# The end of a transformer layer on one core: residual by an identity matmul, copies on ScalarE, and the first FFN1 blocks in halves

## The chip, the cores and the metric

The kernel runs on one core of a Trainium2 chip. That core has five engines that run side by side and meet at semaphores: TensorE (PE in the profile, its weight loads are PEld), VectorE (DVE), ScalarE (ACT), GpSimd (POOL), and SyncE (SP), which issues the DMA transfers here. The metric is device time in microseconds (us), the median of several runs.

## The reference

One layer on x of 2048 tokens by 1024, in bf16: attention with 32 heads of 32, then a feed-forward block of width 3584, each behind a layer norm and each added to its input.

```python
x = A_x
h = x + _A_ref(_layernorm(x, axis=-1), A_wqkv, A_wo)      # attention, then @ wo
h2 = h + _B_ref(_layernorm(h, axis=-1), B_w1, B_b1, B_w2, B_b2)
# _B_ref: gelu(x @ w1 + b1) @ w2 + b2
```

What matters below is the second half for one chunk of tokens: `h = x + attention @ wo`, the layer norm of h, `h @ w1` with gelu (FFN1), and `@ w2` plus h (FFN2).

## The kernel before, in words

**Tiling.** The tokens are handled in four chunks (`qc`) of 512, each of four tiles (`t4`) of 128. Attention of chunk qc runs while the projection by wo, layer norm, FFN1 and FFN2 of chunk qc-1 run as background work of TensorE, in one bank of PSUM (bank 7) and with matmuls in four column strips (line 439). After the attention of the last chunk nothing is left to run beside it: the last chunk's wo, norm, FFN1 and FFN2 come alone, lines 896 to 905. This is the tail. It may use all eight PSUM banks (the list `al`), and its matmuls are whole ones, 128 rows by 128 columns of weights with 512 moving columns (line 443).

**The tail, stage by stage.**

- `finish` (lines 665 to 681): when the last pair of heads is done, VectorE copies the denominators (Dsb, line 666) and the sums (Osb, line 668) out of PSUM, takes reciprocals in four pieces of 128 tokens (line 673), and multiplies (line 677) to give OT, the attention output of head group 7, one piece for each tile of tokens.
- `wo` (lines 703 to 721): for each tile and each half j of the 1024 columns, eight matmuls (one for each head group g) into one bank, then one VectorE addition (line 719) that takes the bank and the tile of x from memory (`b_xr`) and writes `hch`, in bf16.
- `ln2` (lines 723 to 733): for each tile, two statistics instructions (line 487) and one that joins them (489) on VectorE; four small steps on GpSimd (492 to 498: copy, add epsilon, two powers), one small copy on VectorE (493), then the normalization on VectorE (502). Eight transposes on TensorE (508) go to one bank, and one ScalarE copy (512) writes the tile's part of `hnT`.
- `ffn1` (lines 735 to 761): 14 blocks of w1 with 256 columns each, in a ring of four buffers (`b_w1r`); each block gives two groups `fc` of eight matmuls over all 512 tokens. A group needs the `hnT` of all four tiles. Gelu by group: ScalarE adds the bias (751), VectorE squares and multiplies (754, 756), ScalarE takes tanh (758), VectorE makes gT (760). Their buffers are rings of four.
- `ffn2` (lines 763 to 785): for each j and t4, a bias matmul, then 28 matmuls over gT, then one VectorE instruction (782) and the store.

**What sets the order.** The code does not write engine queues by hand. Every instruction becomes a task with a cost and a priority; `Graph.schedule` (lines 98 to 178) plays the tasks through a model of the engines and so fixes the order of each engine's queue, and `assign` (181 to 250) gives each task the semaphore waits that it needs. On the chip each queue runs in that order: an instruction that waits holds up all that stand behind it on its engine. Dependencies are by buffer: `hch` is one buffer for each tile, so its second half is written after the first, and the statistics of a tile wait for both halves.

Of the kernel before, what the change touches and what calls it, by code (L numbers as in the profile page):

```python
# [7 lines left out]
ACT = mybir.ActivationFunctionType  # L8
ALU = mybir.AluOpType
# [3 lines left out]
P = 128  # L13
# [271 lines left out]
def build_kernel(nc, A_x, A_wqkv, A_wo, B_w1, B_b1, B_w2, B_b2, out):  # L285
# [5 lines left out]
    NCH = S // 512  # L291
    G = D // P
    DC = D // P
    FC = F // P
    SCALE = DH ** -0.5
    EPS_BF = 1.0013580322265625e-05
    C2 = 1.0 / 0.044715
    K2 = 2.0 * math.sqrt(2.0 / math.pi) * 0.044715

    x2 = A_x[0]  # L300
# [34 lines left out]
    ident, B_ident = sb(top, "ident", [P, P], BF)  # L335
# [84 lines left out]
    def c_dve_ps(n):  # L420
        return (120 + n) / 960.0 + 0.02

    def c_dve(n, x=1):
        return (62 + n / x) / 960.0 + 0.02
# [7 lines left out]
    def mm(bank, lhsT, rhs, start, stop, reads, narrow, cols=(0, 512)):  # L432

        c0, c1 = cols
        occ = MM * (c1 - c0) / 512.0 + 0.003
        if narrow:
            fns = []
            for j in range(4):
                fns.append(lambda p, j=j: p.matmul(psum[32 * j:32 * j + 32, bank, c0:c1], lhsT[:, 32 * j:32 * j + 32], rhs,  # L439
                                                   start=start, stop=stop, tile_position=(0, 32 * j), skip_group_check=True))  # L440
            pe(fns, occ, reads=reads, writes=[B_ps[bank]], mode="col")
        else:
            pe(lambda p: p.matmul(psum[:, bank, c0:c1], lhsT, rhs, start=start, stop=stop),  # L443
               occ, reads=reads, writes=[B_ps[bank]], mode="full")

    def act(fn, n, reads=(), writes=(), prio=0, ap_bias=False, kind=""):
        return gr.add(E.Activation, fn, c_act(n, ap_bias), 0.14, reads, writes, prio, kind)

    def dve(fn, occ, reads=(), writes=(), prio=0):
        return gr.add(E.DVE, fn, occ, 0.08, reads, writes, prio)  # L450
# [4 lines left out]
    def dma(out_ap, in_ap, nbytes, reads=(), writes=(), prio=0, noncontig=False, after=()):  # L455
        def fn(s):
            if noncontig:
                with nc.allow_non_contiguous_dma(reason="strided gather"):
                    return s.dma_start(out_ap, in_ap)
            return s.dma_start(out_ap, in_ap)  # L460
        return gr.add(E.SP, fn, 0.06, 0.0, reads, writes, prio, nbytes=nbytes, after=after)
# [147 lines left out]
    class Att:  # L609
# [55 lines left out]
        def finish(self, qc, g, pr, bank):  # L665
            dve(lambda v: v.tensor_copy(Dsb[64 * pr:64 * pr + 64, :], psum[64:128, bank, :]), c_dve_ps(512),  # L666
                reads=[B_ps[bank]], writes=B_Dsb[pr], prio=-1)
            dve(lambda v: v.tensor_copy(Osb[64 * pr:64 * pr + 64, :], psum[0:64, bank, :]), c_dve_ps(512),  # L668
                reads=[B_ps[bank]], writes=[B_Osb[pr]], prio=-1)
            self.fin.add((qc, g, pr))  # L670
            if (qc, g, 1 - pr) in self.fin:
                for k in range(4):
                    dve(lambda v, k=k: v.reciprocal(Dsb[:, 128 * k:128 * k + 128], Dsb[:, 128 * k:128 * k + 128]), 0.93,  # L673
                        reads=[B_Dsb[0][k], B_Dsb[1][k]], writes=[B_Dsb[0][k], B_Dsb[1][k]], prio=1)
                    if qc == NCH - 1 and g == G - 1:
                        c = slice(128 * k, 128 * k + 128)
                        dve(lambda v, c=c: v.tensor_tensor(OT[:, qc % 2, g, c], Osb[:, c], Dsb[:, c], ALU.mult), c_dve(128),
                            reads=[B_Dsb[0][k], B_Dsb[1][k]] + B_Osb, writes=[B_OT[qc % 2][g][k]], prio=1)
                if not (qc == NCH - 1 and g == G - 1):
                    dve(lambda v: v.tensor_tensor(OT[:, qc % 2, g, :], Osb[:, :], Dsb[:, :], ALU.mult), c_dve(512),  # L680
                        reads=B_Dsb[0] + B_Dsb[1] + B_Osb, writes=B_OT[qc % 2][g], prio=1)
# [16 lines left out]
    def wblock(R, src_ap, prio=1):  # L698
        s = R.next("w1", R.nw1)
        dma(R.w1[:, s, :, :], src_ap.rearrange("(dc p) c -> p dc c", p=P), P * DC * 512, writes=[R.B_w1[s]], prio=prio)  # L700
        return s

    def wo(R, qc, banks, RX):
        nb = 0
        R.cnt["w1"] += -R.cnt["w1"] % 4
        ws = [wblock(R, A_wo[:, 256 * k:256 * k + 256]) for k in range(4)]
        assert ws == [0, 1, 2, 3]
        for t4 in range(4):
            for j in range(2):
                s = ws[2 * j]  # L710
                bank = banks[nb % len(banks)]
                nb += 1
                tt = qc * 4 + t4
                for k, g in enumerate([7, 0, 1, 2, 3, 4, 5, 6] if len(banks) == 1 else range(G)):
                    mm(bank, OT[:, qc % 2, g, t4 * P:(t4 + 1) * P], R.w1[:, s:s + 2, g, :], k == 0, k == 7,
                       [B_OT[qc % 2][g][t4], R.B_w1[s], R.B_w1[s + 1]], len(banks) == 1)
                x3 = RX.next("x", RX.nx)
                dma(RX.x[:, x3, :], x2[tt * P:(tt + 1) * P, 512 * j:512 * j + 512], P * 1024, writes=[RX.B_x[x3]], prio=1)
                dve(lambda v, t4=t4, j=j, x3=x3, bank=bank: v.tensor_tensor(  # L719
                    hch[:, t4, 512 * j:512 * j + 512], psum[:, bank, :], RX.x[:, x3, :], ALU.add),  # L720
                    c_dve_ps(512), reads=[B_ps[bank], RX.B_x[x3]], writes=[B_hch[t4]])

    def ln2(R, qc, banks, between=None):
        nb = 0
        for t4 in range(4):
            if t4 == 2 and between is not None:
                between()
            s = R.next("xb", R.nxb)
            layer_norm([(hch[:, t4, :], B_hch[t4], R.xb[:, s, :], R.B_xb[s])], 1)
            bank = banks[nb % len(banks)]  # L730
            nb += 1
            transposes(R.xb[:, s, :], R.B_xb[s], bank, R.hnT[:, :, t4 * P:(t4 + 1) * P], R.B_hnT[t4],
                       "dve" if len(banks) == 1 else "act", 0)

    def ffn1(R, qc, banks):
        nb = 0
        for blk in range(FC // 2):
            s = wblock(R, B_w1[:, 256 * blk:256 * blk + 256])
            for f in range(2):
                fc = 2 * blk + f  # L740
                bank = banks[nb % len(banks)]
                nb += 1
                for dc in range(DC):
                    mm(bank, R.w1[:, s, dc, f * P:(f + 1) * P], R.hnT[:, dc, :], dc == 0, dc == DC - 1,
                       [R.B_w1[s]] + R.B_hnT, len(banks) == 1)
                i = R.next("gl", R.ngl)
                if len(banks) == 1:
                    dve(lambda v, i=i, fc=fc, bank=bank: v.tensor_scalar(R.xh[:, i, :], psum[:, bank, :], b1f[:, fc:fc + 1], None, ALU.add),  # L748
                        c_dve_ps(512), reads=[B_ps[bank], B_b1f], writes=[R.B_xh[i]])
                else:  # L750
                    act(lambda a, i=i, fc=fc, bank=bank: a.activation(R.xh[:, i, :], psum[:, bank, :], ACT.Identity,
                                                                      bias=b1f[:, fc:fc + 1], scale=1.0),
                        512, reads=[B_ps[bank], B_b1f], writes=[R.B_xh[i]], ap_bias=True)
                dve(lambda v, i=i: v.tensor_tensor(R.sq[:, i, :], R.xh[:, i, :], R.xh[:, i, :], ALU.mult), c_dve(512, 2),
                    reads=[R.B_xh[i]], writes=[R.B_sq[i]], prio=1)
                dve(lambda v, i=i: v.scalar_tensor_tensor(R.uu[:, i, :], R.sq[:, i, :], C2, R.xh[:, i, :], ALU.add, ALU.mult),
                    c_dve(512), reads=[R.B_sq[i], R.B_xh[i]], writes=[R.B_uu[i]], prio=1)
                act(lambda a, i=i: a.activation(R.th[:, i, :], R.uu[:, i, :], ACT.Tanh, bias=0.0, scale=K2 / 2), 512,
                    reads=[R.B_uu[i]], writes=[R.B_th[i]], prio=-1)
                dve(lambda v, i=i, fc=fc: v.scalar_tensor_tensor(gT[:, fc, :], R.th[:, i, :], 1.0, R.xh[:, i, :], ALU.add, ALU.mult),  # L760
                    c_dve(512), reads=[R.B_th[i], R.B_xh[i]], writes=[B_gT[fc]], prio=1)

    def ffn2(R, qc, banks):
        nb = 0
# [135 lines left out]
    R2.w2, R2.B_w2, R2.nw2, R2.cnt["w2"] = R1.w2, R1.B_w2, R1.nw2, R1.cnt["w2"]  # L900
    R2.hnT, R2.B_hnT = R1.hnT, R1.B_hnT
    wo(R1, NCH - 1, al, R2)
    ln2(R2, NCH - 1, al)
    ffn1(R2, NCH - 1, al)
    ffn2(R2, NCH - 1, al)


# [99 lines left out]
```

## Time and profile before

| what | before |
|---|---|
| median of 3 runs | 1203.71 us |
| lowest, highest | 1203.57, 1204.14 us |
| span of the profiled execution | 1417.9 us |
| mean granted TensorE clock in the profiled execution | 0.749 |
| TensorE, ScalarE, VectorE, GpSimd busy | 96%, 77%, 47%, 3% |
| from the last attention matmul to the end | 1256.8 to 1415.8 us |

The profiled execution has no other time than its span, and the span is 17.8% longer than the median of the runs. The trace says that TensorE was granted three quarters of its clock for nearly all of it. The trace is of that one execution; the runs have no trace.

How to read the views: a row of the chain of waits gives start, duration, engine, what is written and the line, and how many instructions were merged. A row of the timeline adds the shapes and, in square brackets, the engine's idle time before the row and what ended it. A row of the table by stretches gives, for each engine, its busy time and the number of instructions in that stretch, then the granted clock and the traffic of the DMA engines.

### The profile page before, as it was taken

The numbers are of one execution on the slowest core, as the hardware profiler recorded it, in microseconds if no ns is written. First come the engines' busy times: TensorE is split into PE (matmuls) and PEld (weight loads), VectorE is DVE, ScalarE is ACT, GpSimd is POOL, SyncE is SP. The second block draws the span as 40 slices with busy tenths as digits, with TensorE's granted clock in tenths as the row PEclk, the third lists the DMA queues.
The fourth block names the chain that finished last, engine by engine and source line by source line (L and its number), as shares of the span: only waits on it lengthen the run. The fifth ranks groups of instructions, "written<-read, shape, count | busy, mean of one in ns | idle before, by whom it ended". The sixth has DMA issues, their size and how long they took to land.

```text
span 1417.9 us, 37847 instructions
## 1 busy us (share of the span) xinstructions
PE 1366.2 (96%) x17326; PEld 510.9 (36%) x17336; DVE 673.2 (47%) x1165; ACT 1085.3 (77%) x1189; POOL 37.9 (3%) x96
## 2 busy tenths in 40 slices
PE   8999999999999999999999999999999999978999
PEld 5544443433333333332333333333333333324333
DVE  7354444443546774223547762225677612245710
ACT  4778787878888888888888888888988888844500
POOL 2000000000100000000100000000000000001000
PEclk7777777777777777777777777777777777766777
DMA  6800000025343222303342230422323322202222
GB/s 165 224 2 13 28 13 14 13 72 156 101 122 101 76 69 72 124 16 98 107 124 71 83 98 16 124 71 63 107 73 98 102 66 85 87 0 75 74 93 71
DMA packets 165793, 112.29 MB, mean 79 GB/s; under 512 B 25345, under 2 KB 162817, under 8 KB 164866
## 3 DMA queue, kind: packets, MB, share of 16 engines
q1 hardware_dynamic: 165634, 109.87, 26.2%
q8 instruction: 136, 2.23, 0.7%
q14 instruction: 23, 0.19, 0.1%
HBM read 98.58 MB, written 11.27 MB: 77 GB/s over the span
## 4 chain that ended last, share of the span: by engine, by line
PE 91%; ACT 4%; DVE 3%; issue 1%; POOL 1%; DMA 0%; POOLq 0%; DVEq 0%
PE ps L439 48%; PE ps L654 17%; PE ps L634 12%; PE ps L443 10%; ACT PT L643 3%; PE ps L658 2%; PE ps L798 1%; ACT xnT L512 1%; DVE a_xh L748 1%; PE ps L508 1%; DVE V L606 0%; DVE stg L547 0%; DVE Osb L668 0%; DVE Dsb L666 0%; DMA a_w1r<-in_A_wqkv_dram 0%
## 5 line engine op out<-in xcount | busy, mean ns | idle before, releaser
L643 ACT ACTIVATE PT<-ps 128x1024 bf16<-128x1024 f32 x1024 | 989.2, 1025 | 180.5 <-PE ps L634 166.1
L654 PE MATMUL ps<-PT,V 128*32 128x512 bf16 x2048 | 383.4, 457 | 13.7 <-DVE V L606 6.2
L658 PE MATMUL ps<-PT,ones 128*32 128x512 bf16 x2048 | 384.8, 458 | 0.0
L439 PE MATMUL ps<-a_w2r,gT 128*32 128x512 bf16 x2688 | 241.9, 452 | 0.0
L634 PE MATMUL ps<-QT,KT 32*128 32x512 bf16 x2048 | 216.7, 414 | 7.4 <-ACT PT L643 7.3
L439 PE MATMUL ps<-a_hnT,a_w1r 128*32 128x512 bf16 x2688 | 215.2, 454 | 4.0 <-DVE a_xh L748 3.2
L654 PEld LDWEIGHTS ps<-PT,V 128*32 128x32 bf16 x2048 | 103.3, 104 | 143.9 <-issue 89.3
L634 PEld LDWEIGHTS ps<-QT,KT 32*128 32x128 bf16 x2048 | 51.5, 91 | 272.3 <-ACT PT L643 164.5
L439 PE MATMUL ps<-xnT,Wall 128*32 128x512 bf16 x1344 | 111.6, 453 | 7.0 <-ACT xnT L512 4.8
L439 PEld LDWEIGHTS ps<-a_w2r,gT 128*32 128x32 bf16 x2688 | 77.3, 109 | 112.0 <-issue 103.3
L673 DVE RECIPROCAL Dsb<-Dsb 128x128 f32<-128x128 f32 x128 | 115.1, 928 | 1.0
L439 PEld LDWEIGHTS ps<-a_hnT,a_w1r 128*32 128x32 bf16 x2688 | 70.6, 107 | 108.0 <-issue 71.4
L782 DVE SCALAR_TENSOR_TENSOR a_ost<-ps,hch 128x512 bf16<-128x512 f32 x24 | 16.6, 692 | 189.8 <-PE ps L439 189.7
L658 PEld LDWEIGHTS ps<-PT,ones 128*32 128x32 bf16 x2048 | 103.5, 104 | 6.6 <-issue 6.6
L748 DVE TENSOR_SCALAR a_xh<-ps,b1f 128x512 bf16<-128x512 f32 x84 | 63.1, 751 | 81.3 <-PE ps L439 80.2
L666 DVE COPY Dsb<-ps 64x512 f32<-64x512 f32 x64 | 44.4, 694 | 101.5 <-PE ps L658 100.1
L439 PE MATMUL ps<-Wall,xnT 128*32 128x256 bf16 x2048 | 83.8, 314 | 0.0
L547 DVE CAST stg<-ps 128x512 bf16<-128x512 f32 x40 | 27.5, 689 | 89.2 <-PE ps L439 89.2
L443 PE MATMUL ps<-a_hnT,b_w1r 128*128 128x512 bf16 x219 | 64.5, 470 | 2.1 <-ACT a_hnT L512 1.5
L439 PEld LDWEIGHTS ps<-Wall,xnT 128*32 128x32 bf16 x2048 | 57.6, 107 | 22.7 <-issue 11.3
L443 PE MATMUL ps<-a_w2r,gT 128*128 128x512 bf16 x219 | 64.1, 461 | 0.5
L439 PE MATMUL ps<-a_w1r,OT 128*32 128x512 bf16 x768 | 63.1, 453 | 0.8 <-DVE hch L719 0.5
(69 smaller groups left out, 875.5 us busy)
## 6 DMA issues: line engine op xcount, KB each, us to landing
a_w2r<-in_B_w_dram SPq DMA_DIRECT2D x56, 512.0 KB, 4.6
a_w1r<-in_B_w_dram SPq DMA_DIRECT2D x42, 512.0 KB, 3.9
a_w1r<-in_A_wo_dram SPq DMA_DIRECT2D x16, 512.0 KB, 4.7
QT<-q_scratch SPq DMA_DIRECT2D x60, 128.0 KB, 2.8
b_w1r<-in_B_w_dram SPq DMA_DIRECT2D x14, 512.0 KB, 3.8
a_w1r<-in_A_wqkv_dram SPq DMA_DIRECT2D x11, 512.0 KB, 5.1
xrb<-in_A_x_dram SPq DMA_DIRECT2D x16, 256.0 KB, 3.9
Wall<-in_A_wqkv_dram SPq DMA_DIRECT2D x16, 256.0 KB, 5.4
```

The lines of the kernel that those rows point to most:

```text
L439: fns.append(lambda p, j=j: p.matmul(psum[32 * j:32 * j + 32, bank, c0:c1], lhsT[:, 32 * j:32 * j + 32], rhs, start=start, stop=stop, tile ...
L443: pe(lambda p: p.matmul(psum[:, bank, c0:c1], lhsT, rhs, start=start, stop=stop), occ, reads=reads, writes=[B_ps[bank]], mode="full")
L508: pe(lambda p, dc=dc: p.transpose(psb[:, bank, dc * P:(dc + 1) * P], src_ap[:, dc * P:(dc + 1) * P], ident[:]), 0.064, reads=[B_src, B_ide ...
L547: dve(lambda v: v.tensor_copy(stg[:, s, :], psum[:, bank, :]), c_dve_ps(512), reads=[B_ps[bank]], writes=[B_stg[s]])
L634: return p.matmul(psum[:, 2 * u + j, :], KT2[r0:r0 + 32, p16, tc, i, :], QT2[r0:r0 + 32, qs, pr, :], start=True, stop=True, tile_position= ...
L643: act(lambda a, u=u, s=s: a.activation(PT[:, s, :, :], psum[:, 2 * u:2 * u + 2, :], ACT.Exp, bias=0.0, scale=SCALE), 1024, reads=[B_ps[2 * ...
L654: fns.append(lambda p, j=j, h=h: p.matmul(psum[32 * j:32 * j + 32, bank, :], V[:, kt, 32 * h:32 * h + 32], PT[:, s, j, :], start=first, st ...
L658: fns.append(lambda p, j=j: p.matmul(psum[64 + 32 * j:96 + 32 * j, bank, :], ones32[:, :], PT[:, s, j, :], start=first, stop=last, tile_po ...
L666: dve(lambda v: v.tensor_copy(Dsb[64 * pr:64 * pr + 64, :], psum[64:128, bank, :]), c_dve_ps(512), reads=[B_ps[bank]], writes=B_Dsb[pr], p ...
L673: dve(lambda v, k=k: v.reciprocal(Dsb[:, 128 * k:128 * k + 128], Dsb[:, 128 * k:128 * k + 128]), 0.93, reads=[B_Dsb[0][k], B_Dsb[1][k]], w ...
L748: dve(lambda v, i=i, fc=fc, bank=bank: v.tensor_scalar(R.xh[:, i, :], psum[:, bank, :], b1f[:, fc:fc + 1], None, ALU.add), c_dve_ps(512), ...
L782: dve(lambda v, o=o, t4=t4, j=j, bank=bank: v.scalar_tensor_tensor(R.ost[:, o, :], psum[:, bank, :], 0.5, hch[:, t4, 512 * j:512 * j + 512 ...
```

## The change

Only the tail differs. The queues of all engines are the same as before up to the end of the last attention matmuls, and SP's queue is the same to its end.

- `finish`: for the last pair of heads alone, the Osb copy goes to ScalarE.
- `wo` in the tail calls `wo_tail`: after the eight matmuls of a group comes a ninth, with the identity as weights and the tile of x as moving operand, that adds x in PSUM; a ScalarE copy takes the place of VectorE's addition.
- `ln2` in the tail transposes into banks 6 and 7 alone.
- `ffn1` takes its first three blocks (six groups, banks 0 to 5) in halves of 256 tokens: first all six groups for tiles 0 and 1, then all six for tiles 2 and 3. Gelu is moved into a function of its own, unchanged. The other eleven blocks are as before.

```diff
         def finish(self, qc, g, pr, bank):
...
+            if qc == NCH - 1 and g == G - 1 and pr == 1:
+                act(lambda a: a.activation(Osb[64 * pr:64 * pr + 64, :], psum[0:64, bank, :], ACT.Copy), 512,
+                    reads=[B_ps[bank]], writes=[B_Osb[pr]], prio=-1)
+            else:
+                dve(lambda v: v.tensor_copy(Osb[64 * pr:64 * pr + 64, :], psum[0:64, bank, :]), c_dve_ps(512),
+                    reads=[B_ps[bank]], writes=[B_Osb[pr]], prio=-1)
...
+                if RX is not R:
+                    wo_tail(R, RX, qc, t4, j, s, bank)
+                    continue
...
+    def wo_tail(R, RX, qc, t4, j, s, bank):
+        tt = qc * 4 + t4
+        x3 = RX.next("x", RX.nx)
+        dma(RX.x[:, x3, :], x2[tt * P:(tt + 1) * P, 512 * j:512 * j + 512], P * 1024, writes=[RX.B_x[x3]], prio=1)
+        for g in range(G):
+            mm(bank, OT[:, qc % 2, g, t4 * P:(t4 + 1) * P], R.w1[:, s:s + 2, g, :], g == 0, False,
+               [B_OT[qc % 2][g][t4], R.B_w1[s], R.B_w1[s + 1]], False)
+        mm(bank, ident[:, :], RX.x[:, x3, :], False, True, [B_ident, RX.B_x[x3]], False)
+        act(lambda a: a.activation(hch[:, t4, 512 * j:512 * j + 512], psum[:, bank, :], ACT.Copy), 512,
+            reads=[B_ps[bank]], writes=[B_hch[t4]], prio=-1)
...
-    def ffn1(R, qc, banks):
+    def ffn1(R, qc, banks, first_blocks=0):
         nb = 0
-        for blk in range(FC // 2):
+        slots = {}
+        for blk in range(first_blocks):
+            slots[blk] = wblock(R, B_w1[:, 256 * blk:256 * blk + 256])
+        for h in range(2):
+            for fc in range(2 * first_blocks):
+                s, f = slots[fc // 2], fc % 2
+                for dc in range(DC):
+                    mm(banks[fc], R.w1[:, s, dc, f * P:(f + 1) * P], R.hnT[:, dc, 256 * h:256 * h + 256],
+                       dc == 0, dc == DC - 1, [R.B_w1[s]] + R.B_hnT[2 * h:2 * h + 2], False,
+                       cols=(256 * h, 256 * h + 256))
+                if h == 1:
+                    gelu(R, fc, banks[fc], banks)
+        nb = 2 * first_blocks
+        for blk in range(first_blocks, FC // 2):
...
-    ln2(R2, NCH - 1, al)
-    ffn1(R2, NCH - 1, al)
+    ln2(R2, NCH - 1, [6, 7])
+    ffn1(R2, NCH - 1, al, 3)
```

The queues that the planner makes of it, from the last attention matmul on:

- TensorE: 59 matmuls of wo in place of 51 (the identity ones included; groups are complete after 16, 18, 24, 33, 39, 48, 57 and 59 of them, tile by tile, two for each tile); the transposes of tiles 0 and 1; three half matmuls; the transposes of tile 2; 21 half matmuls; the transposes of tile 3; 72 half matmuls; 176 whole ones; FFN2 as before. Before, it was 51 of wo, all 32 transposes, 224 whole ones, FFN2.
- VectorE: copy of Dsb, two reciprocals, two multiplications, again two and two; then tile by tile the statistics, and behind the statistics of tile 1, 2 and 3 the normalization of tile 0, 1 and 2. Before, the eight additions stood between reciprocals, multiplications and statistics.
- ScalarE: the copy of Osb, eight copies of wo's banks, the four copies to hnT, then gelu: the bias instructions of up to three groups stand ahead of the first tanh, and run up to three groups ahead of it after that.
- GpSimd: the four tiles one after the other, where before the first two ran together.

More of the change, by code (lines that the diff above doesn't have):

```diff
@@ L667, in finish @@
                 reads=[B_ps[bank]], writes=B_Dsb[pr], prio=-1)
-            dve(lambda v: v.tensor_copy(Osb[64 * pr:64 * pr + 64, :], psum[0:64, bank, :]), c_dve_ps(512),
-                reads=[B_ps[bank]], writes=[B_Osb[pr]], prio=-1)
+            if qc == NCH - 1 and g == G - 1 and pr == 1:
[4 more added lines that the diff above has]
+                    reads=[B_ps[bank]], writes=[B_Osb[pr]], prio=-1)
             self.fin.add((qc, g, pr))
@@ L745, in ffn1 @@
                        [R.B_w1[s]] + R.B_hnT, len(banks) == 1)
[L746 to L759, printed above, removed]
@@ L760, in ffn1, with gelu @@
-                dve(lambda v, i=i, fc=fc: v.scalar_tensor_tensor(gT[:, fc, :], R.th[:, i, :], 1.0, R.xh[:, i, :], ALU.add, ALU.mult),
-                    c_dve(512), reads=[R.B_th[i], R.B_xh[i]], writes=[B_gT[fc]], prio=1)
+                gelu(R, fc, bank, banks)
+    def gelu(R, fc, bank, banks):
+        i = R.next("gl", R.ngl)
+        if len(banks) == 1:
+            dve(lambda v, i=i, fc=fc, bank=bank: v.tensor_scalar(R.xh[:, i, :], psum[:, bank, :], b1f[:, fc:fc + 1], None, ALU.add),
+                c_dve_ps(512), reads=[B_ps[bank], B_b1f], writes=[R.B_xh[i]])
+        else:
+            act(lambda a, i=i, fc=fc, bank=bank: a.activation(R.xh[:, i, :], psum[:, bank, :], ACT.Identity,
+                                                              bias=b1f[:, fc:fc + 1], scale=1.0),
+                512, reads=[B_ps[bank], B_b1f], writes=[R.B_xh[i]], ap_bias=True)
+        dve(lambda v, i=i: v.tensor_tensor(R.sq[:, i, :], R.xh[:, i, :], R.xh[:, i, :], ALU.mult), c_dve(512, 2),
+            reads=[R.B_xh[i]], writes=[R.B_sq[i]], prio=1)
+        dve(lambda v, i=i: v.scalar_tensor_tensor(R.uu[:, i, :], R.sq[:, i, :], C2, R.xh[:, i, :], ALU.add, ALU.mult),
+            c_dve(512), reads=[R.B_sq[i], R.B_xh[i]], writes=[R.B_uu[i]], prio=1)
+        act(lambda a, i=i: a.activation(R.th[:, i, :], R.uu[:, i, :], ACT.Tanh, bias=0.0, scale=K2 / 2), 512,
+            reads=[R.B_uu[i]], writes=[R.B_th[i]], prio=-1)
+        dve(lambda v, i=i, fc=fc: v.scalar_tensor_tensor(gT[:, fc, :], R.th[:, i, :], 1.0, R.xh[:, i, :], ALU.add, ALU.mult),
+            c_dve(512), reads=[R.B_th[i], R.B_xh[i]], writes=[B_gT[fc]], prio=1)
```

## Prediction

> **What bounds the kernel now.** First the page. TensorE is busy nearly throughout; of the 40 slices only the first, at the start, and the 36th and 37th (1241 to 1312) stand out, and in these two the clock is lower too. They hold the end of attention and the start of the tail, where the whole edit lies.
>
> ```profile
> PE   8999999999999999999999999999999999978999
> ...
> PEclk7777777777777777777777777777777777766777
> ```
>
> Then the chain of waits from the last attention matmul (1256.8) on. TensorE carries it to 1271.1; VectorE, GpSimd and ScalarE carry it for 13 us; TensorE takes it again with FFN1 at 1284.09 and keeps it.
>
> ```profile
> 1256.81 14.26 PE ps L443 x50
> ...
> 1271.89 0.69 DVE hch L719
> 1272.58 1.19 DVE st L487 x2
> ...
> 1274.63 1.04 POOL denb L496 x2
> 1275.67 1.03 POOL rden L498 x2
> ...
> 1280.94 0.56 DVE b_xb L502
> ...
> 1281.54 1.05 PE ps L508 x8
> ...
> 1282.61 1.03 ACT a_hnT L512
> 1283.64 0.45 issue
> 1284.09 6.01 PE ps L443 x15
> ```
>
> The norm of all four tiles ends late, since the statistics of the last ones stand behind all additions, and GpSimd then works them off in 6.9 us (1273.95 to 1280.83). Last, the table by stretches with the granted clock (the number ahead of the DMA share): idleness halves the clock, and FFN1 starts at 0.50.
>
> ```profile
> 1274.00:1276.00 2.00, 0.00 (x0) 0.00 (x0) 2.00 (x8) 0.00 (x0) 2.00 (x7) 0.65 0.00 0
> ...
> 1278.00:1280.00 2.00, 1.49 (x15) 1.23 (x14) 0.61 (x2) 1.80 (x2) 1.75 (x5) 0.50 0.00 0
> ...
> 1286.00:1288.00 2.00, 2.00 (x7) 0.67 (x5) 0.00 (x0) 0.68 (x1) 0.00 (x0) 0.50 0.00 0
> 1288.00:1290.00 2.00, 2.00 (x8) 0.78 (x7) 1.11 (x2) 0.01 (x1) 0.00 (x0) 0.64 0.00 0
> ```
>
> **The change, part by part, at the profile's clock.** I count from t = 0 at 1256.75, the first of 51 wo matmuls that TensorE runs in 14.63 us: 0.284 each (14.63 less the last one's 0.43, over 50).
>
> *Eight identity matmuls.* 59 x 0.284 = 16.8 against 14.5: **2.3 later**. They wait for x, whose loads SP does not show after 1204, so long landed. Head group 7 of tile 0 is wanted as the 15th matmul, at 4.0; VectorE has it at about 0.1 + 0.7 (Dsb) + 1.8 (two reciprocals) + 0.3 = 2.9, with the Osb copy on idle ScalarE beside it. With that copy still on VectorE it would be 3.6, so its move is worth nothing here; the second to fourth tiles are wanted later still.
>
> *Copies on ScalarE.* A 128x512 copy from PSUM took 597 ns there (line 544), VectorE's addition 690 ns (line 719). ScalarE is free: it idled 23.16 us ahead of line 512. Of the eight copies two are on the path: tile 3's halves, complete after 57 and 59 matmuls. With the 0.15 from a group's last matmul to its reader: 16.35 to 16.95, and, behind the first since both write one buffer, 17.05 to 17.65. Queued behind them on ScalarE are the copies to hnT. [...]
>
> *The norm, tile by tile.* VectorE no longer adds, so each tile's statistics can start as its copy ends. Tiles 0 to 2 are complete after 18, 33 and 48 matmuls, 4 us apart; a tile needs about 1.3 (statistics, twice 0.64) + 0.2 (joining) + 2.1 on GpSimd (1278.84 to 1280.83, and the hand-over) + 0.55 (normalization), so GpSimd never piles up. But tile 0's normalization stands behind tile 1's statistics, and tile 2's behind tile 3's: tile 3's statistics 17.7 to 19.0, tile 2's normalization 19.05 to 19.6, tile 3's 22.7.
>
> *FFN1 starts on two tiles.* TensorE transposes tiles 0 and 1 only after wo, into banks 6 and 7, which tile 3 frees at 16.95 and 17.65: eight took 0.71 at 0.75 clock (around 47 us). So 17.0 to 17.7 and 17.7 to 18.4; hnT copies of 1.02, overlapping by 0.1, to 19.7; with the old 0.45, **FFN1 starts at 20.15**, against 1284.09 - 1256.75 = 27.34: 7.2 earlier, the 2.3 included.
>
> *What is queued inside FFN1.* Three half matmuls (0.4), then tile 2's transposes: wanted at 20.6, ready at 19.6. 21 halves later, tile 3's: wanted at 24.3, ready at 22.7. Their 16 transposes now cost TensorE 16 x 0.07 = **1.1**. The halves themselves: 96 of 256 columns carry the columns of 48 whole ones. No such row exists. Below, no gain; above, each would pay a bare weight load, 96 x 0.098 = 9.4; the nearest row excludes that, since transposes load new weights for every 128 columns and still follow at 0.07, the rate of their columns. I take 0.
>
> *The clock.* Before, FFN1 ran at 0.50 from 1284.1 to about 1288.9; that cost 4.8 x (1 - 0.50/0.75) = 1.6. After, TensorE is without dense work from 16.8 to 20.15, and dense only from about 21.3. Between 1238 and 1248 it was 58% to 75% busy and the clock fell only at the end, so 0 to 3.4 us at 0.50 remain likely: 0 to 1.1, and 1.6 if it is as long as before. I take 0.9. The 32 transposes before (1277 to 1283) did not raise the clock: 0.50 in their stretches. [...]
>
> *Beside other work.* Queue order on SP is unchanged. FFN2 is as before. w1 buffers 0 to 2 are held until the second halves, but block 4 is wanted 32 halves and 16 whole ones (9 us) after buffer 0 is freed, and a block lands in 3.8.
>
> **Sum** at the profile's clock: 7.2 - 1.1 + 1.6 - 0.9 = **6.8 us**, 1417.9 to 1411.1; bounds 6.1 and 7.7 by the clock term.
>
> **From the profile to the runs.** The span is 17.8% above the median, so the runs had a faster clock than 0.75; which, nothing shows. The other end is 1.00 (an estimate, matmul times scaled from these rows). Wo then ends at 10.9 before and 12.6 after. Before, VectorE's additions end at 12.7 (15.83 in the profile), and the chain behind them keeps its length: FFN1 at 24.2. After, the same steps as above from 12.6 give 16.0: 8.2 earlier. Transposes 0.85; the clock before 4.8 x 0.5 = 2.4, after 1.0: 8.2 - 0.85 + 1.4 = 8.75. Between 6.8 and 8.75 I take 7.5: **1196.2 us**.
>
> **The rivals.**
>
> *A, the clock stays halved longer.* The three halves, transposes and hnT waits make a scattered start, as the 46% to 75% activity after 1238 did, and two more stretches of 3.4 us run at 0.50. For: the fall at 1248 under partial work. Against: it rose at 1254 with equally partial work. Price 2 x 1.1 to 2 x 1.7, about 3: gain 4.5, **1199.2**.
>
> *B, gelu becomes the bound: slower.* The six first groups reach VectorE only after the first halves; then it owes 28 groups without a break. At 1.00 clock the first arrives at about 24.1, and FFN2 wants the last gT 30 matmuls after FFN1's end: 65.5 + 6.5 = 72. That allows 1.71 a group. VectorE's three rows are 425, 692 and 685 ns, 1.80 in sum, 1.68 by their starts (1298.12, 1298.73 and the 0.46 ahead), so the margin is nil. If the waits between ScalarE and VectorE, whose bias instructions now stand ahead of older tanh, stretch a group to the 2.28 it took before (when TensorE set the pace), the last gT is at 88: 16 late, 16 - 8.75 = 7 lost, **1211**. It decides against the change from 2.0 a group at 1.00; at 0.75 the allowance is 2.26, so there it costs nothing. Near 2.0 it ends as no change.
>
> *C, the norm comes late.* Tile 2's transposes have 1.0 us to spare and tile 3's 1.6 (0.5 and 0.35 at 1.00), and all FFN1 stands behind them. If GpSimd's four steps or the extra semaphore hand-overs take 1.5 to 2.5 more for each, the gain is 5: **1198.7**. Against: those steps are measured.
>
> *D, the change does not shorten what the runs wait for.* If in the runs the gap before was shorter than in the profile, say because the clock did not fall, 2.4 of the 8.75 go, and 6.3 are left: still faster, 1197.4, inside the forecast's range.
>
> **How the numbers follow.** Forecast with D 0.63; A 0.15; C 0.08; B 0.14, half of it near its break-even. About 0.2% (2.4 us) is what a measurement of this kernel can tell from no change. Faster: 0.63 + 0.15 + 0.08 = 0.86; same 0.07; slower 0.07. The range goes from 1193.2 (8.75, the clock not falling at all, another 1.0, and 0.7 of spread between runs) to 1200.4, which takes in A and C and leaves out B and their far ends.
>
> **What would show it.** FFN1's first matmul about 20 us after the end of attention, not 27; the additions of line 719 gone from VectorE between the reciprocals and the statistics; wo's matmuls without a gap, 59 in 16.8; half matmuls at 0.14; no wait of TensorE for the normalization of tiles 2 and 3. The prediction is wrong if TensorE idles inside FFN1 or at FFN2's start for gT (B), if the clock column shows 0.50 for more than 4 us after FFN1's start (A), or if half matmuls follow at 0.2 or more at 0.75 clock.

## The result and the profile after

The changed kernel takes **1196.48 us** (median of four runs, 1193.62 to 1198.45), the kernel before beside it 1203.91 (median of four, 1203.57 to 1204.14; below, each ratio is to runs of before made beside the kernel in question): a ratio of **0.9937, 95% interval 0.9923 to 0.9951**, 7.4 us faster. The prediction said 1196.2, of a range of 1193.2 to 1200.4.

The profiled execution of before had TensorE at a mean clock of 0.749 and that of the changed kernel at 0.993; the timed runs had 0.986 to 0.997 wherever their clock was recorded. So before was profiled again (the first experiment below, clock 0.987), and it is with that trace that the changed one is compared. The page of the changed kernel, TensorE's busy share and clock in 40 slices:

```profile
PE   7899999999999999998999999999999999989998
PEclk9999999999999999999999999999999999989999
```

Of the two slices of low activity near the end only the 36th (1047 to 1077, the end of attention) is left, at 8 in both rows. The 37th, 1077 to 1107, in which the edit lies, now reads 9 in both; in the repeated profile of before it reads 7 and 7.

The chain of waits of the changed kernel, from the end of attention on (start, length, engine, tile, line):

```profile
1075.61 10.48 PE ps L443 x48
...
1086.12 0.60 ACT hch L738
...
1086.74 0.70 DVE st L487
...
1088.17 0.45 DVE b_xb L502
...
1088.80 0.62 PE ps L508 x8
...
1089.44 1.95 ACT a_hnT L512 x2
...
1091.44 0.50 PE ps L443 x3
1091.94 0.77 PE ps L508 x8
1092.70 3.63 PE ps L443 x21
1096.34 0.45 PE ps L508 x8
1096.78 67.44 PE ps L443 x348
...
1164.24 6.76 DMA a_w2r<-in_B_w_dram
...
1171.05 22.63 PE ps L443 x104
```

ScalarE's copy (line 738) stands where VectorE's addition stood, GpSimd is gone from the chain, and TensorE enters FFN1 at 1091.44 on the tiles 0 and 1 alone, then takes tile 2's transposes, 21 halves, tile 3's transposes, without a wait. A late transfer of w2 is new in it. All stretches below are counted from t = 0, the start of the unbroken run of wo matmuls that opens the tail (here 1075.61). So FFN1 starts at 15.83, and the last VectorE operation ends at 118.86.

The same kernel by stretches (TensorE busy second, granted clock ahead of the DMA share):

```profile
1090.00:1092.00 2.00, 0.56 (x7) 0.53 (x8) 1.42 (x5) 1.38 (x2) 1.00 (x4) 0.98 0.00 0
1092.00:1094.00 2.00, 2.00 (x15) 1.57 (x14) 0.55 (x1) 1.02 (x1) 1.07 (x2) 0.50 0.01 4
1094.00:1096.00 2.00, 2.00 (x14) 1.56 (x13) 0.00 (x0) 0.00 (x0) 0.00 (x0) 0.67 0.00 0
```

The clock halves just behind FFN1's start and comes back at 1095.3 (by stretches of 0.5 us: 1091.91 to 1095.32).

### The profile page after: what moved, and what is told of

It reads as the page before. It is cut to its first block, busy times and chain, and to the rows that moved or that the text cites. A ratio compares the mean times of both kernels' runs of the same rounds, so it can differ in the third digit from the quotient of the medians.

```text
span 1196.7 us, 37982 instructions
## 1 busy us (share of the span) xinstructions
PE 1130.4 (94%) x17392; PEld 469.8 (39%) x17392; DVE 660.9 (55%) x1156; ACT 1065.4 (89%) x1198; POOL 37.7 (3%) x96
## 4 chain that ended last, share of the span: by engine, by line
PE 74%; ACT 11%; DVE 11%; DMA 2%; issue 1%; SPq 1%; DVEq 0%
PE ps L439 41%; PE ps L654 13%; PE ps L634 11%; ACT PT L643 10%; PE ps L443 9%; DVE a_xh L782 3%; DVE a_uu L790 1%; ACT xnT L512 1%; DVE gT L794 1%; DVE Dsb L677 1%; DVE Dsb L666 1%; DVE Osb L672 1%; SPq L460 1%; DVE stg L547 1%; DMA a_w2r<-in_B_w_dram 1%
## 5 line engine op out<-in xcount | busy, mean ns | idle before, releaser
L643 ACT ACTIVATE PT<-ps 128x1024 bf16<-128x1024 f32 x1024 | 967.6, 1035 | 32.6 <-PE ps L634 19.0
L654 PE MATMUL ps<-PT,V 128*32 128x512 bf16 x2048 | 318.8, 384 | 14.2 <-DVE V L606 5.3
L658 PE MATMUL ps<-PT,ones 128*32 128x512 bf16 x2048 | 318.8, 384 | 0.0
L439 PE MATMUL ps<-a_w2r,gT 128*32 128x512 bf16 x2688 | 199.7, 381 | 0.0
L439 PE MATMUL ps<-a_hnT,a_w1r 128*32 128x512 bf16 x2688 | 174.4, 381 | 10.8 <-DVE a_xh L782 9.9
L439 PE MATMUL ps<-xnT,Wall 128*32 128x512 bf16 x1344 | 92.6, 386 | 8.6 <-ACT xnT L512 5.5
L439 PE MATMUL ps<-Wall,xnT 128*32 128x256 bf16 x2048 | 68.4, 273 | 0.1
L794 DVE SCALAR_TENSOR_TENSOR gT<-a_th,a_xh 128x512 bf16<-128x512 f32 x84 | 56.7, 675 | 3.2 <-ACT a_th L792 2.7
L790 DVE SCALAR_TENSOR_TENSOR a_uu<-a_sq,a_xh 128x512 bf16<-128x512 bf16 x84 | 56.7, 678 | 1.4
L792 ACT ACTIVATE a_th<-a_uu 128x512 f32<-128x512 bf16 x84 | 52.9, 634 | 1.9 <-DVE a_uu L790 1.3
```

What stands on the lines that cost most here:

```text
L643: act(lambda a, u=u, s=s: a.activation(PT[:, s, :, :], psum[:, 2 * u:2 * u + 2, :], ACT.Exp, bias=0.0, scale=SCALE), 1024, reads=[B_ps[2 * ...
L654: fns.append(lambda p, j=j, h=h: p.matmul(psum[32 * j:32 * j + 32, bank, :], V[:, kt, 32 * h:32 * h + 32], PT[:, s, j, :], start=first, st ...
L658: fns.append(lambda p, j=j: p.matmul(psum[64 + 32 * j:96 + 32 * j, bank, :], ones32[:, :], PT[:, s, j, :], start=first, stop=last, tile_po ...
```

## The experiments

**Before, at the clock of the runs.** The kernel before, profiled again.

> The unchanged kernel, for a trace at the clock of the runs (the first trace had 0.749, the changed kernel's 0.993). The theory: the attention of the last chunk ends at the same time as with the change (1075.6), and the whole difference lies behind it. Counted from that end, FFN1 starts at 24.2 by the estimate on record (15.8 was measured with the change), about 5 us of its start run at half the clock, and from the end of attention to the end of the program 126 to 127 us pass, against 118.9 with the change. Rival: the phases ahead of the tail differ too (another end of attention by over 2 us), so that part of the gain comes from there.

Measured: 1202.79 us, span 1201.0, clock 0.987. Its chain of waits:

```profile
1072.83 9.19 PE ps L443 x42
...
1085.24 1.19 DVE st L487 x2
...
1092.98 0.59 POOLq L941
...
1093.60 0.56 DVE b_xb L502
...
1094.21 1.05 PE ps L508 x8
...
1095.28 1.03 ACT a_hnT L512
1096.31 0.45 issue
1096.76 13.17 PE ps L443 x49
```

FFN1 starts 23.93 us after wo's start, the tail ends at 125.97, and the clock is 0.50 from 1088.03 to 1101.68, the first 4.9 us of FFN1 included. Against the changed kernel the tail is 7.11 longer. That is nearly the 7.4 of the runs. Attention ended 2.8 us earlier in this execution (1072.83 against 1075.61), so in this pair none of the gain comes from ahead of the tail. Over all twelve profiles at the clock of the runs attention ends between 1071.1 and 1075.6: before at 1072.83 and 1072.85, the changed kernel at 1075.61 and 1073.68. So single executions differ by up to 4.5 us ahead of the tail, where the queues are the same, and it is the tails that are compared here.

**Each part alone.** The residual on TensorE with the copies on ScalarE, FFN1 whole; and the halves alone, with the residual added on VectorE. The first:

```diff
-    ln2(R2, NCH - 1, [6, 7])
-    ffn1(R2, NCH - 1, al, 3)
+    ln2(R2, NCH - 1, al)
+    ffn1(R2, NCH - 1, al)
```

> One part alone: residual by the identity matmul and copies on ScalarE in the tail, as in the change; the first FFN1 blocks are whole and the transposes use all eight banks, as before. The theory says that the parts add up: tile 3 of the norm was ready 18.1 us after the end of attention in the changed kernel, so all transposes and hnT copies end at about 20 and FFN1 starts at 20.3, without transposes inside it. That is 3.3 later than the changed kernel's 15.8 + 1.2 of transposes, and FFN1 starts at half the clock for 3.4 to 5 us, about 0.7 more than in the changed kernel: gain over before 3 to 4 us of its 7.4. Rival 1: the faster norm is the whole gain and the halves only pay back their own transposes: gain 6 or more. Rival 2: without halves the identity matmuls cost as much as they bring: gain under 1.

Measured: 1201.25 us against 1202.02, ratio 0.9986 (0.9975 to 0.9996). FFN1 starts at 20.86, where 20.3 was expected, and the tail ends at 123.19. The second:

```diff
-            if qc == NCH - 1 and g == G - 1 and pr == 1:
+            if False:
...
-                if RX is not R:
+                if False:
```

> The other part alone: the first three FFN1 blocks in halves and transposes in two banks, as in the change; additions stay on VectorE, no identity matmul, the Osb copy on VectorE. TensorE's queue then holds the transposes of tiles 0 to 2, ten half matmuls, the transposes of tile 3, the rest. In the first trace tile 2's transposes ended at 1280.5 and FFN1 started at 1284.1, so FFN1 starts 3.5 us earlier, less 0.6 for tile 3's transposes inside it. The theory: gain over before 2.5 to 3.5 us, and with the residual alone about the whole 7.4. Rival: the halves bring nothing unless the norm is faster, because tile 3 is as late as before and the pieces in between run at half the clock: gain under 1.

Measured: 1200.0 us, ratio 0.998 (0.9968 to 0.9992). TensorE in its timeline (start, length, what; in brackets the idle time ahead and what ended it):

```profile
1090.62 1.89 PE L508 MATMUL ps<-ident,b_xb 128*128 128x128 bf16 x16 [5.91 <-DVE b_xb L502]
1093.09 1.03 PE L508 MATMUL ps<-ident,b_xb 128*128 128x128 bf16 x8 [0.59 <-DVE mvr L493]
1093.91 2.34 PE L443 MATMUL ps<-a_hnT,b_w1r 128*128 128x256 bf16 x10
1096.05 1.06 PE L508 MATMUL ps<-ident,b_xb 128*128 128x128 bf16 x8
```

Tiles 0 and 1 are still normalized so late that TensorE waits 5.91 us for them. The halves begin with tile 2's transposes done, at 20.3 (t = 0 is 1073.59), and spare only the wait for tile 3; the tail ends at 122.32. What follows: FFN1 starts 3.1 and 3.6 us earlier by the parts and 8.1 by both. With the residual alone tiles 0 and 1 are ready early and FFN1 waits for tile 3 all the same; with the halves alone FFN1 could start on two tiles, but VectorE's additions still hold up their statistics, and GpSimd still works the tiles off late. In the tails the parts save 2.8 and 3.7 (3 to 4 and 2.5 to 3.5 were expected) against 7.1, so they nearly add up; in the medians 0.8 and 2.0 against 7.4, with intervals of 0.5 to 3.0 and 1.0 to 3.8. Neither part alone explains the gain.

**The clock kept up in the changed kernel.** Sixteen filler matmuls behind wo, whose result nobody reads:

```diff
     ln2(R2, NCH - 1, [6, 7])
+    for k in range(16):
+        pe(lambda p: p.matmul(psum[:, 5, 0:256], ident[:, :], b2t[:, 0:256], start=True, stop=True), 0.11,
+           reads=[B_ident, B_b2t], writes=[B_ps[5]], kind="warm")
```

> The changed kernel with 16 matmuls of 256 columns more, whose result is not used (identity weights, into a bank that FFN1 clears later), put where TensorE idles between the end of wo and FFN1's start. In the changed kernel's trace the clock fell to 0.50 at about 1092 and rose at about 1094.7, in the first FFN1 halves. If that fall is the answer to the idle stretch of 1088.5 to 1091.4, the clock stays at 1.00 and the gain over the changed kernel is 2.7 x 0.5 = 1.3 us (1.0 to 1.7), 8.7 over before, with runs less scattered. Rival: the fillers stand ahead of FFN1's first matmuls, or the clock falls anyway: 0 to 1.5 us slower than the changed kernel.

Measured: 1193.07 us against 1202.02, ratio 0.9923 (0.9906 to 0.9939). TensorE in its timeline:

```profile
1083.79 0.60 PE L939 MATMUL ps<-b2t,ident 128*128 128x256 bf16 x4
1084.30 0.61 PE L508 MATMUL ps<-ident,b_xb 128*128 128x128 bf16 x8
...
1085.37 1.36 PE L939 MATMUL ps<-b2t,ident 128*128 128x256 bf16 x11
1086.93 0.39 PE L443 MATMUL ps<-a_hnT,b_w1r 128*128 128x256 bf16 x2 [0.20 <-ACT a_hnT L512]
...
1087.61 2.56 PE L443 MATMUL ps<-a_hnT,b_w1r 128*128 128x256 bf16 x22
```

The clock stays at 1.00, FFN1 starts at 15.82 as without fillers, and the tail ends at 116.27: 2.6 less. Of these 0.8 are the wait for w2, which this execution does not have; the other 1.8 are the clock (3.41 us at half speed lose 1.7).

**The clock kept up in before.** 78 fillers in the same manner behind line 903 of before; TensorE runs 57 of them right behind wo.

```diff
     ln2(R2, NCH - 1, al)
+    for k in range(78):
+        pe(lambda p: p.matmul(psum[:, 5, 0:256], ident[:, :], b2t[:, 0:256], start=True, stop=True), 0.13,
+           reads=[B_ident, B_b2t], writes=[B_ps[5]], kind="warm")
```

> The kernel before, with 78 filler matmuls of 256 columns in TensorE's idle stretch between wo and FFN1 (57 of them right behind wo). The prediction put 1.4 of its 8.75 us at full clock down to the clock: 2.4 lost before, 1.0 after. If the clock costs before about as much as it cost the changed kernel (there the fillers took 2.6 us off the tail), then here the granted clock stays at 1.00, FFN1 begins about 23.5 us after the start of wo (23.9 without fillers), and the tail falls from 126.0 to 123.1 to 123.6 us: 1199.2 us (1198.5 to 1200.5), and the clock's share of the gain is about 0. If before lost nothing to the clock, or the transposes wait behind the fillers, the time stays at 1202 (1201 to 1203).

Measured: 1199.82 us against 1203.19, ratio 0.9975 (0.9963 to 0.9988). TensorE in its timeline:

```profile
1083.80 6.39 PE L905 MATMUL ps<-b2t,ident 128*128 128x256 bf16 x57
...
1092.34 0.62 PE L508 MATMUL ps<-ident,b_xb 128*128 128x128 bf16 x8 [0.50 <-DVE mvr L493]
...
1096.02 2.33 PE L443 MATMUL ps<-a_hnT,b_w1r 128*128 128x512 bf16 x10 [0.79 <-ACT a_hnT L512]
```

The last of these lines is FFN1's start, at 23.17 (t = 0 is 1072.85). The clock stays at 1.00 and the tail ends at 122.56, 3.4 less than before without fillers (0.2 of it a wait for w2): 0.76 from the transposes and what stands around them, 2.5 from FFN1's first 4.9 us. So at an equal clock of 1.00 the order of the work alone is worth 122.56 - 116.27 = **6.3 us**, and the clock has a share of its own: it costs before about 3.2, and the changed kernel 1.8 when it falls there. The expectation, that the two lose alike, does not hold.

**The sums on VectorE.** The changed kernel with the copy of Osb back on VectorE.

```diff
-            if qc == NCH - 1 and g == G - 1 and pr == 1:
+            if False:
```

> The changed kernel, but the last copy of the attention sums (Osb) goes back to VectorE. The prediction held its move to ScalarE to be worth nothing. In the profile of the changed kernel tile 0 of head group 7 is ready about 2.75 us after the start of the unbroken wo matmuls (its product begins at 1078.07, the start is 1075.61); 0.7 more makes 3.45, and with 18 matmuls of 0.2155 ahead of it TensorE wants it at 3.9. So no wait of TensorE in wo, and FFN1 still begins 15.8 us (15.6 to 16.1) after that start. Rival: the copy delays every later step of VectorE, and FFN1 begins 0.7 later, at 16.5, or wo has a gap.

Measured in one execution: 1192.67 us, FFN1 at 15.83 (1088.21, t = 0 at 1072.38). VectorE and then TensorE in its timeline:

```profile
1073.16 0.68 DVE L672 COPY Osb<-ps 64x512 f32<-64x512 f32 x1
...
1077.95 1.42 DVE L487 BATCH_NORM_STATS2 st<-hch 128x6 f32<-128x512 bf16 x2
```

```profile
1085.57 1.16 PE L508 MATMUL ps<-ident,b_xb 128*128 128x128 bf16 x16 [0.35 <-DVE mv L489]
1088.21 0.50 PE L443 MATMUL ps<-a_hnT,b_w1r 128*128 128x256 bf16 x3 [1.48 <-ACT a_hnT L512]
...
1088.99 2.46 PE L443 MATMUL ps<-a_hnT,b_w1r 128*128 128x256 bf16 x21
```

Tile 0's statistics begin 0.7 later (5.57 against 4.92), wo has no gap, and FFN1 starts when it did. The move of this copy is worth nothing. The clock did not fall here, though TensorE's gap is the same; 21 halves then take 2.46 in place of 3.84.

**One block in halves and not three.**

```diff
-    ffn1(R2, NCH - 1, al, 3)
+    ffn1(R2, NCH - 1, al, 1)
```

> The changed kernel with one FFN1 block in halves and not three: 32 half matmuls in place of 96, the rest whole. Theory: halves cost nothing of themselves (they follow at 0.108 us for 256 columns), and three blocks are there to cover the norm of tiles 2 and 3. With one block TensorE has 16 first halves to cover it, takes tile 3's transposes about 1.0 us earlier and then stands idle for one copy to hnT, about 1.1 us (0.8 to 1.6): a wait of that size for tile 3's hnT in the trace, and a tail of 119.5 to 120.5 us where the changed kernel has 118.9. Rival: the 64 halves fewer save their own overhead, 0.02 or more each, 1.3 us, and the tail is 118.5 or less in spite of the wait.

Measured: 1194.99 us (1192.91 to 1196.28), ratio 0.9931 (0.9914 to 0.9948). TensorE in its timeline:

```profile
1089.61 1.58 PE L443 MATMUL ps<-a_hnT,b_w1r 128*128 128x256 bf16 x13
1091.31 0.62 PE L508 MATMUL ps<-ident,b_xb 128*128 128x128 bf16 x8
1093.05 5.16 PE L443 MATMUL ps<-a_hnT,b_w1r 128*128 128x256 bf16 x31 [1.11 <-ACT a_hnT L512]
```

The wait for tile 3's copy is there, 1.11 against 1.1 expected. The tail, 118.42, lies under the expected 119.5 to 120.5 and where the rival put it; but it is not to be held against 118.86, since the clock did not fall in this execution. Against 116.23, the tail with the sums on VectorE, where the clock stayed up too, it is 2.2 longer: 1.1 this wait, 0.5 a wait for w2, and 0.4 a wait for tile 3's normalization, which the row of its weight loads shows; 0.2 is unassigned.

```profile
1091.31 0.45 PEld L508 LDWEIGHTS ps<-ident,b_xb 128*128 128x128 bf16 x8 [0.39 <-DVE b_xb L502]
```

So the halves pay no overhead that fewer of them would save, and it takes more than one block to cover the norm of tile 3; yet in the runs the difference between one block and three is not seen.

**Gelu made longer, once and twice.** The square in the last chunk's gelu is computed a second time, and in a second kernel a third time, to move rival B's point.

```diff
             reads=[R.B_uu[i]], writes=[R.B_th[i]], prio=-1)
+        if len(banks) > 1:
+            dve(lambda v, i=i: v.tensor_tensor(R.sq[:, i, :], R.xh[:, i, :], R.xh[:, i, :], ALU.mult), c_dve(512, 2),
+                reads=[R.B_xh[i], R.B_uu[i]], writes=[R.B_sq[i]], prio=1)
```

> The changed kernel with a fourth VectorE operation for each of the 28 gelu groups of the last 512 tokens: the square is computed twice (419 ns), the output is the same. It tests rival B's place. In the changed kernel the starts of the last operation of a group lie 1.54 us apart (1103.5 to 1145.2 over 27 groups), and the last gT is ready at 1145.9, where FFN2, which began at 1142.47, wants it 28 matmuls of 0.219 later, at 1148.6: 2.7 to spare. With 1.90 to 1.96 a group the last gT is 10 to 11 later, so TensorE loses 7 to 8.5 us waiting for gT or for banks, and the whole gain is gone: 1204 us (1202 to 1206). If VectorE is not what FFN2 waits for, or has more to spare than this, the time stays within 2 us of the changed kernel, 1196 to 1198.5.

Measured: 1196.63 us (1195.26 to 1198.6), ratio 0.9952 (0.9933 to 0.9971); the expected loss of 8 us did not come. The changed kernel and the longer one, the last operation of all groups (shortest, median and longest in ns, then the first and the last start):

```profile
L794 DVE SCALAR_TENSOR_TENSOR gT<-b_th,b_xh x28: 681/684/691, 1103.5 to 1145.2; 128x512 bf16<-128x512 f32 x28
```

```profile
L797 DVE SCALAR_TENSOR_TENSOR gT<-b_th,b_xh x28: 683/696/699, 1099.9 to 1149.6; 128x512 bf16<-128x512 f32 x28
```

A group takes 41.7 / 27 = 1.54 in the changed kernel and 1.84 here, and the last gT comes at 1150.3. It was to be wanted after 28 matmuls of FFN2. But the planner, which knows the longer gelu, put the last four matmuls of FFN2's first tile behind 24 of the second: the first tile's output is evicted at 1151.91 and the second's at 1152.78, where the changed kernel has 1149.36 and 1155.18. So the last gT was in time by 1.2 us.

> The changed kernel with two more VectorE operations for each gelu group (the square computed three times, the output the same), to find the point from which rival B decides. One more made a group 1.84 us (1099.9 to 1149.6 over 27), put the planner's last four matmuls of FFN2's first tile behind 24 of the second, and left the last gT 1.2 us to spare (ready at 1150.27, wanted at 1151.5), so nothing was lost. Another 0.30 a group makes 2.14, and the last gT comes 8 us later: 6.9 late. Rival B's mechanism: TensorE waits for gT or for banks, 5 to 8 us in all, and the time is 1200 to 1204.5. If the planner finds cover again, as it did for one more operation, TensorE waits under 2 us and the time stays at 1195 to 1198.5.

Measured: 1204.43 us (1203.1 to 1207.21) against 1202.39, ratio 1.0015 (1.0005 to 1.0024): slower than before. Its waits of TensorE in the tail, and its timeline:

```profile
PE ps L443 <- ACT b_xh L785: 5.8, 3, 3.0
```

```profile
1149.23 0.61 PE L443 MATMUL ps<-b2t,two_row 128*128 128x512 bf16 x1 [2.95 <-ACT b_xh L785]
1149.63 6.92 PE L443 MATMUL ps<-a_w2r,gT 128*128 128x512 bf16 x24
```

Two groups take 4.42 us in its chain, 2.21 each, and TensorE waits 5.8 us for banks that gelu still holds. The waits have a second price: the clock falls to 0.50 from 1145.99 to 1152.81, so that the 24 matmuls take 6.92 us, where 24 took 5.34 in the changed kernel. The tail is 126.02, 7.2 longer than the changed kernel's 118.86: 5.8 of waits and 1.6 of clock, less the 0.8 for w2, which is not waited for here; 0.6 is unassigned. Rival B's mechanism exists; with the clock's part it decides somewhere between 1.84 and 2.21 a group, and the changed kernel stands at 1.54.

**The changed kernel and the one with fillers, once more side by side.**

> The changed kernel again, beside the one with fillers on the same chip. In its first profile the clock fell for one stretch of 3.41 us at FFN1's start, 16.30 us after the start of the unbroken wo matmuls; in three other profiles with the same gap (the sums on VectorE, the longer gelu, the one block in halves) it did not fall. Theory: the fall hangs on how the gap lies to a grid of 3.41 us, so it comes in some executions only. Then this one's tail is either near 118 (fall, 0.50 for 3.4 us) or near 116.3 (no fall), apart from waits for w2, and the median is 1194 to 1197.5. Rival: the fall is sure in this program, and what spared the three others is their own edit: then the tail is near 118 again.

> The changed kernel with 16 filler matmuls of 256 columns behind wo, again, beside the changed kernel itself. If only a part of the changed kernel's executions lose 1.7 to the clock, the fillers are worth 0 to 1.8 us in the median, about 1: 1193 to 1196 where the changed kernel has 1194 to 1197.5, and the tail in the profile is 116.3 again, the clock at 1.00. If the fall is sure, they are worth 1.7 to 2.6.

Measured: 1196.0 us (1194.29 to 1198.35) and 1195.03 (1192.52 to 1197.68), ratios to before 0.9947 (0.9935 to 0.9959) and 0.9938 (0.9926 to 0.995). The clock of the changed kernel fell again, from 1089.98 to 1093.40, just behind FFN1's start at 1089.51:

```profile
1090.00:1092.00 2.00, 2.00 (x16) 1.62 (x13) 0.55 (x1) 1.02 (x1) 1.12 (x2) 0.50 0.00 0
```

That fits the theory and the rival alike, so this pair does not decide between them (the last section says what the traces add). Its tail is 118.47 with 0.5 of waiting for w2, that of the one with fillers 116.31, the clock at 1.00. The fillers save the tail 2.2 in this pair of profiles and 2.6 in the first, but the medians differ by 1.0 here, and the intervals overlap: that the version with fillers beats the changed kernel is likely and not shown. It beats before in both series.

## Why the prediction was right

Point by point, with its steps at full clock, since the runs had nearly that.

- **Wo and the identity matmuls.** Ends at 10.9 and 12.6 were predicted; 11.1 and 12.84 came, in the trace of before and the changed one. No gap in wo. The move of Osb is worth nothing, as said (shown by undoing it).
- **Copies on ScalarE, the norm tile by tile.** The copies took 597 ns each, as the row of line 544 had it. Tile 2's normalization was done 0.59 us before TensorE asked for it (1091.18 against 1091.77; 0.5 predicted); tile 3's 0.8 where the clock stayed up (1090.50 against 1091.29, with the sums on VectorE; 0.35 predicted). Rival C is out.
- **FFN1's start.** 24.2 and 16.0 predicted, 23.93 and 15.83 measured: 8.1 earlier, against 8.2.
- **Transposes inside FFN1.** 0.85 predicted; 0.45 for each eight at full clock in the chain, 0.9.
- **Halves at no cost.** 22 halves in 2.56 us at 1.00 (the version with fillers), less the 0.27 that one matmul of this size shows by itself, are 0.109 each over 21, half of a whole one's 0.218 (48 in 10.48 in wo). Right.
- **The clock.** Before loses 2.46 in FFN1 (4.92 us at half speed), predicted 2.4. The changed kernel loses 1.7 (3.41 at half speed) where 1.0 was taken, with a bound of 0 to 3.4 us. It fell in both of its profiles and in the one with the longest gelu, and not in three others with the same gap. Rival A, more than 4 us at 0.50, came in none of the six. Its argument misread the rows: TensorE was busy 58% to 75% of the stretches ahead of the fall at 1248, and 79% to 88% of those ahead of the rise at 1254, so not equally. The last section orders these executions by how long TensorE was busy in one step of 3.41 us, transposes counted. Before lost more than the prediction's term: 3.2 by the fillers, 0.76 of it ahead of FFN1, which the prediction carried inside the chain.
- **Not in the sum.** FFN2 waits for a w2 transfer at 1171.05, 0.8 us in the changed kernel's profile, 0.5 in its second, 0.2 in before's, and none with fillers or with the sums on VectorE. "FFN2 is as before" left it out; what makes these transfers late in some executions stays open.
- **Rival B.** The price of a group was set too high: 1.68 by the starts and 1.80 by the sum, where the traces show 1.54. The last gT was ready at 1145.9 and wanted at 1148.7. Its break-even of 2.0 fits the two longer gelus, and the planner has cover that the working did not see.
- **Rival D.** Out: at the clock of the runs before has its gap in full, 23.93 us up to FFN1, and the clock fell in it.

The sum as measured: 8.1 - 0.9 + 2.46 - 1.7 - 0.6 (the wait for w2 over before's) = 7.4; read directly, the tails differ by 7.11. That the forecast of 7.5 lay so near was luck. It was set between the two clocks, 1.25 under the 8.75 of full clock, although the runs had full clock; and the full sum happened to be too high by about as much, 0.7 for the clock after and 0.6 for w2. The mechanism was right; these two are the terms that were mis-sized.

## What to carry to other kernels

When a serial chain of small steps on other engines stands between two dense stages, let the next stage start on the part that is ready, and take away what keeps that part from being ready early; here each alone took 2.8 and 3.7 us off the tail (0.8 and 2.0 off the median of the runs), and both together 7.1 (7.4). Then price the other side of the bargain, the engine that now has less time to deliver: VectorE's gelu had room from 1.54 to over 1.84 us a group, and at 2.21 the whole gain was gone. And count the clock of the matrix engine as a term of its own, for it gave part of the gain here: 1.4 us where the clock falls in the changed kernel too, 3.2 where it holds.

## What the runs showed of the hardware

In these traces the changes of the clock lie whole steps of 3.41 us apart. In the changed kernel's profile it rises at 1074.84, falls at 1091.91 and rises at 1095.32: 17.07 and 3.41 us apart, five steps and one. In before it is down from 1088.03 to 1101.68, four steps of 3.41. The edges of these steps, counted on from the clock's last rise ahead of the tail, lie differently to the tail in each execution. One lay 16.30 us behind wo's start in both profiles of the changed kernel, and the clock fell there; one lay at 14.8 and 14.9 in those with the longer gelu and the one block in halves, and the clock held, with the same gap of 0.35 and 1.3 to 1.5 idle around the transposes up to FFN1's start. With the sums on VectorE one lay at 16.43 and the clock held too; with the longest gelu, whose edit is of the same kind as the longer one's, one lay at 16.23 and the clock fell.

What orders these executions is how long TensorE was busy in the step of 3.41 us ahead of the edge, transposes counted. One step each of the changed kernel, of the sums on VectorE and of the halves alone (length, busy time and instructions of TensorE, then the clock):

```profile
1088.50:1091.91 3.41, 1.63 (x22) 1.00 0.00 0
```

```profile
1085.40:1088.81 3.41, 1.76 (x24) 1.00 0.00 0
```

```profile
1083.46:1086.87 3.41, 1.25 (x6) 1.00 0.00 0
```

A fall followed in the first and the third, none in the second. Falls in the tail followed steps with 0 us busy (before), 0.59 (the longest gelu, waiting for banks), 1.25 (halves alone), 1.45 (residual alone), 1.63 and 1.69 (the changed kernel) and 1.64 (the longest gelu); the least busy steps without a fall had 1.76 (sums on VectorE) and 2.3 (one block in halves). So the author's reading is that the fall hangs on how the gap lies to the steps; in this tail a fall followed every step at full clock with up to 1.69 us busy of 3.41, and none with 1.76 or more. This order needs the transposes counted. The first and the second step hold the same 16 transposes of tiles 0 and 1 and the same three half matmuls; the second only has five of tile 2's transposes ahead of the edge where the first has three. And without its transposes the second, where the clock held, has 0.50 us busy (its three half matmuls), less than the 1.25 of the third, where it fell. Two reservations: the order rests on one execution just above it, and on ends of matmuls that the profile models. It also holds for this tail alone; toward the end of attention, whose matmuls are narrower (weights of 128x32 and 32x128), falls followed steps of up to 2.00 us. The longest idle stretch of TensorE between wo's end and the fall in the changed kernel was 1.48 us.
